# TensorE kept in program order from step 20 on, global softmax moved one and two steps forward

## The chip, the cores and the metric

One core of one Trainium2 chip. The metric is the device time of one execution in microseconds (us), lower is better. The kernel before was measured three times: 1033.65 us median, 1033.2 to 1033.82.

## The reference

Window attention for 8 batches of 8 heads (512 local and 32 global positions, head size 64), then a two-layer FFN (512 to 2048 to 512) with a squared ReLU, in float32:

```python
s_g = scale * np.matmul(q_g, k_all.transpose(0, 1, 3, 2))      # global rows see all 544 keys
out_g = np.matmul(sm(s_g), v_all)
s_ll = np.where(mask, scale * np.matmul(q_l, k_l.transpose(0, 1, 3, 2)), -1e9)   # |i - j| <= 32
a_l = sm(np.concatenate([scale * np.matmul(q_l, k_g.transpose(0, 1, 3, 2)), s_ll], axis=-1))
out_l = np.matmul(a_l, np.concatenate([v_g, v_l], axis=2))
x = np.concatenate([out_g, out_l], axis=2)                     # then to (batch * seq, 512)
h = x @ w_in
r = np.maximum(h, 0.0)
return (s * (r * r) + b) @ w_out
```

## The kernel before, in words

Most operands are split into a high and a low part in the matmul format fp32r, and a product is the sum of three (high by high, high by low, low by high). The work is a software pipeline of 138 steps (the loop at L617). A **head** step `j` (0 to 127) is one head of one half of one batch: 16 steps make a batch, 8 steps make a **tile** of 256 rows of x. An **FFN** step `m = j - 10` takes an eighth of the hidden layer of tile `m // 8`. So step `j` issues, in program order:

- `sp(j+1)`, `ld(j+2)`, `vl(j)`: the splits of K and Q of the next head (L201 to L204, on ScalarE, VectorE and GpSimd) and the loads. K and Q of two heads share one buffer, so in odd steps two copies of K and one or two of Q come together.
- `sc(j)`: four score products into `ps_s` (L383), one for the global queries into `ps_g` (L389), the softmax (L224 on VectorE, L230 on ScalarE, L233 to L240 on VectorE) and the eviction of `ps_g` (L393, L394).
- `early`: in two steps of each batch four transposes of global probabilities into `ps_tg` (L462), evicted by L465 on ScalarE and L466 on VectorE.
- `ffn_in(m)`: 24 products into `ps_h` (L532), then L538, L539, L546, L547 make the hidden values `g` from it.
- `transposes_and_pv(j-1, j-2)`: four transposes into `ps_t` (L324, evicted by L399 and L400) between four products of probabilities and V into `ps_o` (L410, evicted by L421, L422, L424 into the tile `x`).
- `extra`: global softmax (L446 to L451), global V loads (L471) and global products (`g_pv`, ten L484).
- `x_split` (L504, L505) in the last step of a tile, in two halves; the second half of the tile is needed by the seventh and eighth product of `ffn_in` in the next step.
- `ffn_out(m-1)`: 12 products into the two accumulators (L564); after eight of them the tile is copied (L572) and stored.
- `late`: the fifth global transpose of a group (L462 again).

The PSUM tag `t` has one buffer: `ps_t`, `ps_tg` and `ps_xg` take turns in it, and each has to be evicted by ScalarE and VectorE before the next is written. `ps_h` has two buffers; the tags `s`, `g` and `o` have one. The SBUF tag `r` has two, shared by `r`, the stored tiles `o` and the loads `xgr`.

The 17th tile is the global rows. They are written to DRAM by `g_pv` and read back by `xg_split` (L512, two loads of 256 rows, transposed by L515, evicted by L517 and L518), which the program places right behind `ffn_in(127)` and ahead of `ffn_out(126)`.

The loop order is not the engines' order: a scheduler that plays the program on its own cost model orders the instructions of each engine, and moves an instruction forward when its inputs are ready in that model. It is entered by

```python
with _tile.TileContext(nc, schedule_with_timeline_sim=True) as tc:
```

and the steps at which the global softmax of the two groups of four heads is issued, and what follows it, are set by

```python
G_AT = (13, 18)
G_TR = 3
G_LD = (0, 2)
G_PV = (1, 3)
```

so that group `g` of batch `b` has its softmax in step `16*b + G_AT[g]`, its transposes three steps later and its two `g_pv` one and three steps after those.

Of the kernel before, what the change touches and what calls it, by code (L numbers as in the profile page):

```python
# [48 lines left out]
LAG = 10  # L49
# [5 lines left out]
SPOTS = ["xs0", "xs1", "kq", "kq"] * 2 + ["xs1", "kq", "kq"] * 2 + ["xs1", "kq"]  # L55
LOADS_AT = {0: (0, 1), 1: (2, 3), **{j: (j + 2,) for j in range(2, 14)}}
BY_HALVES = 2
NORM_ACT = lambda j: j < 0
X_ACT = lambda j: j >= 8
G_AT = (13, 18)  # L60
G_TR = 3
G_LD = (0, 2)
G_PV = (1, 3)
# [9 lines left out]
def window_attention_then_ffn(ctx: ExitStack, tc: tile.TileContext, qd, qg, kw, vw, vg, qz, qgz, vz, w_in, w_out, sv, bv, out):  # L73
# [63 lines left out]
    def weight_load(k):  # L137
        st = ops.tile([P, 2048], I32, tag=SPOTS[k], name=f"wst{k}", bufs=1 + (SPOTS[k] == "kq"))
        staged[k] = st
        sources = (w_in[k], w_out[k * P:(k + 1) * P, :])  # L140
        for i in range(2):
            queue = nc.scalar if k == 0 else nc.sync
            queue.dma_start(st[:, 1024 * i:1024 * (i + 1)], sources[i])

    def weight_chunk(k):
        st = staged.pop(k)
        n = 2 if k < BY_HALVES else 1
        for i in range(n):
# [66 lines left out]
    def softmax(j, p_s):  # L215
# [19 lines left out]
        for blk in range(2):  # L235
            p = sm[:, cols[blk]]
            if NORM_ACT(j):
                nc.scalar.activation(out=p, in_=p, func=AF.Copy, scale=ss[:, blk:blk + 1])
# [203 lines left out]
    def g_softmax(b, g):  # L442
        v = st_["sg", b, g]
        gm = sb.tile([P, 2], F32, tag="gm", name=f"gm{b}_{g}", bufs=1)
        gm, gs = gm[:, 0:1], gm[:, 1:2]
        nc.vector.reduce_max(out=gm, in_=v, axis=mybir.AxisListType.X)  # L446
        nc.vector.tensor_scalar_mul(gm, gm, -scale)
        nc.scalar.activation(out=v, in_=v, func=AF.Exp, bias=gm, scale=scale, accum_out=gs)
        nc.vector.tensor_scalar_add(gs, gs, 1e-9)
        nc.vector.reciprocal(gs, gs)  # L450
        nc.vector.tensor_scalar_mul(v, v, gs)  # L451
# [132 lines left out]
    NM = NT * 8  # L584
    extra, early, late = defaultdict(list), {}, {}
    for b in range(B):
        for g in range(2):
            s0 = 16 * b + G_AT[g]
            extra[s0].append(lambda b=b, g=g: g_softmax(b, g))
# [23 lines left out]
    piece, last = 0, None  # L613
    qg_load(0)
    ld(0)
    ld(1)
    for j in range(NM + LAG + 2):  # L617
        sp(j + 1)
        ld(j + 2)
        vl(j)  # L620
        for k in LOADS_AT.get(j, ()):
            weight_load(k)
        if j < 16:
            weight_chunk(j)
            piece += 1
        if j < NS:
            b1 = j // 16 + 1
            if j == 14 and NF > 16:
                qg_load32(1)
            elif j % 16 == 14 and b1 < B:  # L630
                qg_load(b1)
            sc(j)
            if j == NF - 1 and NF % 16:
                if NF > 16:
                    qg_load(j // 16)
                qg_split(j // 16)
            if j % 16 == 15 and NF <= j + 1 < NS:
                qg_split(b1)
        if j in early:
            early.pop(j)()  # L640
        m = j - LAG if LAG <= j < NM + LAG else None
        if m is not None:
            ffn_in(m)
            if m == 8 * 15 + 7:
                xg_split(16)
        tr(j - 1)
        transposes_and_pv(j - 1, j - 2)
        vsp(j - 1)
        for fn in extra.pop(j, []):
            fn()  # L650
        pvs(j - 2)
        vl32(j)
        if j in SPLIT_AT:
            x_split(SPLIT_AT[j])
        if last is not None:
            ffn_out(last)
        last = m
        if j in late:
            late.pop(j)()
    assert piece == 16 and not extra  # L660


# [76 lines left out]
```

## Time and profile before

| what | value |
|---|---|
| median of three runs | 1033.65 us |
| time of the profiled execution | 1033.77 us |
| its span in the trace | 1032.0 us |
| TensorE matmul busy | 1009.5 us (98%), 7100 instructions |
| VectorE, ScalarE busy | 801.1 us (78%), 712.3 us (69%) |
| GpSimd busy | 314.7 us (30%) |
| mean granted TensorE clock | 0.993 |

Around the span lie 1.77 us that the trace doesn't show. Matmuls are pipelined: the duration of one is longer than the distance to the next, so distances between starts are the measure of what a product costs.

### The profile page before, as it was taken

How to read it: one execution, taken by the hardware profiler on the slowest of the kernel's cores; microseconds unless marked ns; L12 is line 12 of the kernel's file. 1: busy time of each engine (PE TensorE's matmuls, PEld its weight loads, DVE VectorE, ACT ScalarE, POOL GpSimd, SP SyncE). 2: the span in 40 equal slices, each digit the busy share in tenths (PEclk: the TensorE clock that was granted, in tenths of full speed). 3: DMA queues.
4: the chain of work that ended last, by engine and by line, in shares of the span. 5: the costliest groups of instructions: out<-in, count | busy, mean ns of one | idle time of the engine just before them, and what ended most of it. 6: DMA issues, size and time to landing. Idle time of an engine off the chain costs nothing.

```text
span 1032.0 us, 20335 instructions
## 1 busy us (share of the span) xinstructions
PE 1009.5 (98%) x7100; PEld 915.7 (89%) x7100; DVE 801.1 (78%) x2069; ACT 712.3 (69%) x1775; POOL 314.7 (30%) x365
## 2 busy tenths in 40 slices
PE   9799999999999999999999999999999999999996
PEld 4589999999999899999999999999999989999895
DVE  5899778988799688988799788988799788954321
ACT  7899767867687667867687667868687667844231
POOL 0003233424244234424244234424343234301000
PEclk9899999999999999999999999999999999999999
DMA  8874312312132122312132122312132212201000
GB/s 332 280 260 161 101 51 72 103 48 92 50 109 76 44 73 72 103 48 91 52 107 78 58 64 67 111 40 93 61 98 77 65 57 68 70 1 49 22 21 21
DMA packets 63534, 88.88 MB, mean 86 GB/s; under 512 B 7624, under 2 KB 48584, under 8 KB 63432
## 3 DMA queue, kind: packets, MB, share of 16 engines
q1 hardware_dynamic: 63144, 86.54, 26.3%
q8 instruction: 56, 0.92, 0.4%
q10 hardware_dynamic: 288, 1.05, 0.3%
q14 instruction: 46, 0.38, 0.1%
HBM read 78.12 MB, written 9.44 MB: 85 GB/s over the span
## 4 chain that ended last, share of the span: by engine, by line
PE 87%; ACT 5%; DVE 4%; DMA 2%; issue 1%; SPq 0%; POOL 0%; ACTq 0%; POOLq 0%; DVEq 0%
PE acc L564 36%; PE ps_h L532 33%; PE ps_t L324 5%; PE ps_o L410 4%; PE ps_s L383 4%; PE ps_og L484 2%; ACT sm L230 1%; PE ps_g L389 1%; DMA wst<-in_w_in 1%; DVE sm L240 1%; PE ps_tg L462 1%; PE ps_o L348 1%; ACT wup L158 1%; ACT wst L159 1%; ACT kq L201 0%
## 5 line engine op out<-in xcount | busy, mean ns | idle before, releaser
L532 PE MATMUL ps_h<-xst,w_all 128*128 128x256 f32 x3264 | 437.4, 281 | 4.0 <-ACT xst L504 1.7
L564 PE MATMUL acc<-w_all,g 128*128 128x512 f32 x1632 | 426.9, 397 | 0.0
L532 PEld LDWEIGHTS ps_h<-xst,w_all 128*128 128x128 f32 x3264 | 407.3, 188 | 14.5 <-DVE r L539 2.3
L564 PEld LDWEIGHTS acc<-w_all,g 128*128 128x128 f32 x1632 | 289.7, 188 | 49.1
L212 POOL TENSOR_TENSOR vs<-rv,vs 128x256 fp32r<-128x256 f32 x112 | 85.7, 765 | 274.0 <-ACT vs L211 262.8
L204 POOL TENSOR_TENSOR kq<-rq,kq 128x256 fp32r<-128x256 f32 x112 | 97.7, 872 | 167.2 <-ACT kq L203 159.1
L539 DVE SCALAR_TENSOR_TENSOR r<-ps_h,s_t,r 128x512 f32<-128x512 f32 x136 | 101.2, 744 | 59.7 <-ACT r L538 59.3
L538 ACT ACTIVATE r<-ps_h 128x512 f32<-128x512 f32 x136 | 81.3, 597 | 80.3 <-PE ps_h L532 74.2
L546 ACT ACTIVATE g<-r,b_t 128x512 fp32r<-128x512 f32 x136 | 98.9, 727 | 50.9 <-DVE r L539 49.3
L547 DVE SCALAR_TENSOR_TENSOR g<-r,b_t,g 128x512 fp32r<-128x512 f32 x136 | 106.5, 783 | 33.7 <-ACT g L546 29.9
L230 ACT ACTIVATE sm<-sm,nm 128x224 f32<-128x224 f32 (+1 forms) x256 | 118.6, 467 | 18.8 <-DVE nm L224 17.5
L224 DVE CUSTOM_DVE_ANT_0 sm<-ps_s,mask 128x224 f32<-128x224 f32 (+1 forms) x256 | 85.0, 366 | 19.6 <-PE ps_t L324 10.2
L202 POOL TENSOR_TENSOR kq<-rk,kq 64x416 fp32r<-64x416 f32 x56 | 67.2, 1199 | 106.5 <-DMA wst<-in_w_out 84.6
L324 PE MATMUL ps_t<-ident,sm 128*128 128x128 f32 x512 | 95.4, 279 | 1.7 <-ACT pt L334 1.5
L240 DVE TENSOR_SCALAR sm<-sm,nm 128x224 f32<-128x224 f32 (+1 forms) x256 | 93.4, 405 | 3.7
L410 PE MATMUL ps_o<-pt,vs 128*128 128x256 f32 x448 | 83.3, 280 | 0.0
L476 POOL TENSOR_TENSOR vsg<-rvg,vsg 128x320 fp32r<-128x320 f32 x64 | 57.5, 918 | 75.7 <-ACT vsg L475 75.6
L383 PE MATMUL ps_s<-kq 128*128 128x192 f32 (+1 forms) x448 | 76.4, 276 | 0.6 <-DVE nm L224 0.6
L399 ACT CAST pt<-ps_t 128x416 fp32r<-128x416 f32 x112 | 57.3, 511 | 24.2 <-PE ps_t L324 23.5
L383 PEld LDWEIGHTS ps_s<-kq 128*128 128x128 f32 x448 | 67.4, 190 | 6.2 <-DVE nm L224 0.8
L393 ACT COPY tg<-ps_g 32x256 f32<-32x256 f32 (+1 forms) x112 | 42.2, 377 | 44.1 <-PE ps_g L389 41.8
L394 DVE TENSOR_TENSOR sg<-ps_g,tg 32x256 f32<-32x256 f32 (+1 forms) x112 | 48.1, 429 | 29.7 <-ACT tg L393 23.1
(71 smaller groups left out, 1218.4 us busy)
## 6 DMA issues: line engine op xcount, KB each, us to landing
rq<-in_qd SPq DMA_DIRECT2D x112, 128.0 KB, 2.1
rv<-in_vw SPq DMA_DIRECT2D x112, 128.0 KB, 2.0
rk<-in_kw SPq DMA_DIRECT2D x64, 208.0 KB, 2.5
rvg<-in_vg SPq DMA_DIRECT2D x32, 320.0 KB, 3.0
out<-o SPq DMA_DIRECT2D x34, 256.0 KB, 2.3
wst<-in_w_in SPq DMA_DIRECT2D x15, 512.0 KB, 4.1
wst<-in_w_out SPq DMA_DIRECT2D x15, 512.0 KB, 5.7
rv<-in_vz SPq DMA_DIRECT2D x16, 256.0 KB, 4.6
```

The costliest lines, as they stand in the source:

```text
L204: nc.gpsimd.tensor_sub(out=qs[:, 1, :], in0=rq, in1=f32(qs[:, 0, :]))
L212: nc.gpsimd.tensor_sub(out=vs[:, :, 1, :], in0=rv4, in1=f32(vs[:, :, 0, :]))
L230: nc.scalar.activation(out=p, in_=p, func=AF.Exp, bias=nm[:, blk:blk + 1], scale=-1.0, accum_out=ss[:, blk:blk + 1],)
L240: nc.vector.tensor_scalar(out=p, in0=p, scalar1=ss[:, blk:blk + 1], scalar2=1.0, op0=ALU.mult, op1=ALU.mult,)
L324: nc.tensor.transpose(out=p_t[:, at:at + P], in_=sm[:, c0:c0 + P], identity=ident)
L383: nc.tensor.matmul(p_s[:, cols], lhsT=qs[:, a, blk * P:(blk + 1) * P], rhs=ks[:, cols], start=(a == 0), stop=(a == 1),)
L410: nc.tensor.matmul(p_o[:, blk, :, q0:q0 + n], lhsT=vs[:, 2 * blk + c], rhs=pt[:, :, o], start=(c == 1), stop=(c == 0),)
L532: nc.tensor.matmul(p_h[:, k], lhsT=wi[:, a, f, c], rhs=xs[:, e, c, :], start=(n == 0), stop=(n == 11),)
L539: nc.vector.scalar_tensor_tensor(out=r, in0=p_h, scalar=s_t, in1=r, op0=ALU.mult, op1=ALU.mult)
L546: nc.scalar.activation(out=g[:, 0], in_=r, func=AF.Identity, bias=b_t)
L547: nc.vector.scalar_tensor_tensor(out=g[:, 1], in0=r, scalar=b_t, in1=f32(g[:, 0]), op0=ALU.add, op1=ALU.subtract,)
L564: nc.tensor.matmul(oacc[t][i], lhsT=g[:, a, k, i * P:(i + 1) * P], rhs=wo[:, e, f, :], start=(pr == 0 and n == 0), stop=(pr == 7 and n == 5),)
```

## The change

Two things. First, `G_AT` becomes `(12, 16)`: the softmax of the first group of a batch and all that hangs on it come one step earlier, those of the second group two steps. Second, from step 20 on all that a step puts on TensorE keeps the order in which the program writes it; the other engines' orders are still made by the scheduler. A product no longer passes one that the program wrote ahead of it. No instruction is added or removed. In the changed file the lines behind L57 have numbers higher by one.

```diff
+ORDERED_FROM = 20
-G_AT = (13, 18)
+G_AT = (12, 16)
...
-    for j in range(NM + LAG + 2):
+    def step(j):
+        nonlocal piece, last
         sp(j + 1)
         ld(j + 2)
         vl(j)
...
+
+    for j in range(ORDERED_FROM):
+        step(j)
+    with tc.manual_schedule(engines={mybir.EngineType.PE}):
+        for j in range(ORDERED_FROM, NM + LAG + 2):
+            step(j)
```

The order of TensorE around the four global transposes of a batch's first group, before. The first number in a name is its step: `ps_s49` are the scores of head 49, `ps_h38` the hidden products of FFN step 38 (in step 48), `ps_o46` the products with V of head 46; `ps_tg2_0_0` are the first four transposes of batch 2, group 0, `ps_tg2_0_4` the fifth, and `ps_t46` and `ps_t47` the transposes of heads 46 and 47, which need the same buffer:

```order
L462 MATMUL ps_tg2_0_0_4448<-ident_58,sg32_2796 128x128 x4
L532 MATMUL ps_h38_4455<-xst4_3823,w_all_60 128x256 x8
L410 MATMUL ps_o46_4486<-pt46_4398,vs46_4401 128x256
L410 MATMUL ps_o46_4486<-pt46_4398,vs46_4401 128x2x96
L410 MATMUL ps_o46_4486<-pt46_4398,vs46_4401 128x256
L410 MATMUL ps_o46_4486<-pt46_4398,vs46_4401 128x2x64
L564 MATMUL acc4_0_4020<-w_all_60,g37_4381 128x512 x6
L564 MATMUL acc4_1_4021<-w_all_60,g37_4381 128x512 x6
L383 MATMUL ps_s49_4538<-kq48_4321 128x192 x2
L383 MATMUL ps_s49_4538<-kq48_4321 128x224 x2
L532 MATMUL ps_h39_4558<-xst4_3823,w_all_60 128x256 x4
L324 MATMUL ps_t47_4489<-ident_58,sm47_4337 128x128 x4
```

The same four transposes now:

```order
L390 MATMUL ps_g47_4337<-kq46_4136,qgs2_2703 64x288
L463 MATMUL ps_tg2_0_0_4356<-ident_58,sg32_2817 128x128 x4
L533 MATMUL ps_h37_4363<-xst4_3825,w_all_60 128x256 x24
L411 MATMUL ps_o45_4394<-pt45_4305,vs45_4308 128x256
L411 MATMUL ps_o45_4394<-pt45_4305,vs45_4308 128x2x96
L325 MATMUL ps_t46_4397<-ident_58,sm46_4247 128x128 x2
L411 MATMUL ps_o45_4394<-pt45_4305,vs45_4308 128x256
L411 MATMUL ps_o45_4394<-pt45_4305,vs45_4308 128x2x64
L325 MATMUL ps_t46_4397<-ident_58,sm46_4247 128x128 x2
L565 MATMUL acc4_0_4022<-w_all_60,g36_4288 128x512 x6
L565 MATMUL acc4_1_4023<-w_all_60,g36_4288 128x512 x6
L463 MATMUL ps_tg2_0_4_4433<-ident_58,sg32_2817 128x128
```

They now stand in step 47, ahead of all 24 hidden products; before they stood in step 48, ahead of the last 8 of 24. The next transposes into their buffer are now those of head 46, two products with V behind the run of 24, and the fifth global transpose stands right behind the run of 12. Before, the next ones (head 47) came behind four products with V, a run of 12, four scores and four hidden products.

On ScalarE the eviction of those four transposes (`pg2_0`, from `ps_tg2_0_0`), before:

```order
L546 ACTIVATE g37_4381<-r37_4378,b_t_88 128x512
L393 COPY tg48_4443<-ps_g48_4431 32x256
L230 ACTIVATE sm48_4433,nm48_4434<-sm48_4433,nm48_4434 128x192
L230 ACTIVATE sm48_4433,nm48_4434<-sm48_4433,nm48_4434 128x224
L465 CAST pg2_0_4447<-ps_tg2_0_0_4448 128x16x32
L538 ACTIVATE r38_4480<-ps_h38_4455 128x512
```

and now:

```order
L394 COPY tg47_4349<-ps_g47_4337 32x288
L373 CAST qgs3_4352<-rqg3_4238 128x8x32
L202 CAST kq50_4555<-rk50_4441 64x416
L204 CAST kq50_4555<-rq50_4443 128x256
L202 CAST kq50_4555<-rk50_4441 64x416
L231 ACTIVATE sm47_4339,nm47_4340<-sm47_4339,nm47_4340 128x224
L466 CAST pg2_0_4355<-ps_tg2_0_0_4356 128x16x32
L231 ACTIVATE sm47_4339,nm47_4340<-sm47_4339,nm47_4340 128x192
L449 ACTIVATE sg36_3269,gm2_1_4536<-sg36_3269,gm2_1_4536 128x544
```

Before, it followed both exponentials (L230) of head 48, an even head. Now it follows the first exponential of head 47, an odd one, with the copy of the next batch's global queries (L373 of the changed file) and three copies of K and Q (L202, L204) between it and the eviction of `ps_g47`.

On TensorE at the end of tile 15, where the global rows come back from DRAM (`ps_xg0`, `ps_xg1`), before:

```order
L532 MATMUL ps_h127_13201<-xst15_12784,w_all_60 128x256 x24
L564 MATMUL acc15_0_12912<-w_all_60,g126_13169 128x512 x6
L564 MATMUL acc15_1_12913<-w_all_60,g126_13169 128x512 x6
L515 MATMUL ps_xg0_13235<-ident_58,xgr0_13233 128x128 x4
L564 MATMUL acc15_0_12912<-w_all_60,g127_13229 128x512 x2
L564 MATMUL acc15_1_12913<-w_all_60,g127_13229 128x512 x2
L564 MATMUL acc15_0_12912<-w_all_60,g127_13229 128x512 x4
L564 MATMUL acc15_1_12913<-w_all_60,g127_13229 128x512 x4
L515 MATMUL ps_xg1_13244<-ident_58,xgr1_13242 128x128 x4
L532 MATMUL ps_h128_13263<-xst16_13232,w_all_60 128x256
```

and now:

```order
L533 MATMUL ps_h127_13203<-xst15_12800,w_all_60 128x256 x24
L516 MATMUL ps_xg0_13237<-ident_58,xgr0_13235 128x128 x4
L516 MATMUL ps_xg1_13246<-ident_58,xgr1_13244 128x128 x4
L565 MATMUL acc15_0_12929<-w_all_60,g126_13188 128x512 x6
L565 MATMUL acc15_1_12930<-w_all_60,g126_13188 128x512 x6
L533 MATMUL ps_h128_13265<-xst16_13234,w_all_60 128x256 x24
L565 MATMUL acc15_0_12929<-w_all_60,g127_13231 128x512 x6
```

Both groups of transposes of global rows now stand in a row behind `ps_h127`, ahead of the products of `g126`; before, the products of `g126` and `g127` stood ahead of and between them.

## The prediction

> **What bounds the kernel now.** I read the page first: span, busy times and the chain that ended last.
>
> ```profile
> span 1032.0 us, 20335 instructions
> PE 1009.5 (98%) x7100; PEld 915.7 (89%) x7100; DVE 801.1 (78%) x2069; ACT 712.3 (69%) x1775; POOL 314.7 (30%) x365
> PE 87%; ACT 5%; DVE 4%; DMA 2%; issue 1%; SPq 0%; POOL 0%; ACTq 0%; POOLq 0%; DVEq 0%
> ```
>
> TensorE is busy for 98% of the span and carries 87% of the chain, so what counts is TensorE's own time and the little that it waits. Next come the waits of TensorE and its timeline. Once in 16 steps it stops for a moment at the first products of a tile (us in total, times, longest); two of its rows there, three batches apart, also measure a batch (start, duration, and in brackets the idle time ahead of it):
>
> ```profile
> PE ps_h L532 <- DVE r L539: 1.1, 7, 0.2
> ```
>
> ```profile
> 303.00 2.78 PE L532 MATMUL ps_h<-xst,w_all 128*128 128x256 f32 x22 [0.17 <-DVE r L539]
> ```
>
> ```profile
> 650.45 1.80 PE L532 MATMUL ps_h<-xst,w_all 128*128 128x256 f32 x13 [0.16 <-DVE r L539]
> ```
>
> Three batches take 650.45 - 303.00 = 347.45, or 115.8 us each, and of such waits there are seven in the whole trace, 1.1 us together: before, TensorE almost never waits in the middle. Now the steps that already stand in program order, 46 and 47 (scores, hidden products, products with V, run of 12, next scores):
>
> ```profile
> 319.42 0.58 PE L383 MATMUL ps_s<-kq 128*128 128x224 f32 x4
> ...
> 326.34 0.58 PE L383 MATMUL ps_s<-kq 128*128 128x224 f32 x4
> 326.76 0.30 PE L389 MATMUL ps_g<-kq,qgs 128*64 128x288 f32 x1
> 326.90 2.91 PE L532 MATMUL ps_h<-xst,w_all 128*128 128x256 f32 x24
> 329.64 0.38 PE L410 MATMUL ps_o<-pt,vs 128*128 128x256 f32 x2
> 329.86 0.38 PE L324 MATMUL ps_t<-ident,sm 128*128 128x128 f32 x2
> ...
> 330.41 3.00 PE L564 MATMUL acc<-w_all,g 128*128 128x512 f32 x12
> 333.24 0.60 PE L383 MATMUL ps_s<-kq 128*128 128x192 f32 x4
> ```
>
> They take 6.92 and 6.90 us from scores to scores.
>
> **The change, part by part.** *Runs in place of mixtures.* From step 20 on every head step looks like these two. The rest of a batch is four groups of ten global products and ten global transposes:
>
> ```profile
> 354.35 0.76 PE L484 MATMUL ps_og<-vsg,pg 128*64 128x128 f32 x10
> 354.95 0.45 PE L532 MATMUL ps_h<-xst,w_all 128*128 128x256 f32 x2
> ```
>
> ```profile
> 335.64 0.60 PE L462 MATMUL ps_tg<-ident,sg 128*128 128x128 f32 x4
> 335.99 1.19 PE L532 MATMUL ps_h<-xst,w_all 128*128 128x256 f32 x8
> ```
>
> Ten products take 0.60, four transposes 0.35 (0.09 each). A batch in order is 16 x 6.91 + 4 x 0.60 + 10 x 0.09 = 113.9. The first product behind such a group comes late by nothing to 0.11 (no row shows all cases), for six groups nothing to 0.7; I take 0.3: 114.2. That is 1.6 less than 115.8. Steps 20 to 127 are 6.75 batches: **-10.9 us** (-8.2 to -12.8), the small waits of before being in it. It holds while TensorE finds its inputs ready, and in program order it has nothing else to do when one is late. So I looked for buffers that the order asks for early.
>
> *One buffer for three kinds of transposes.* In step 16b+15 four global transposes go ahead of the 24 hidden products, and the four of a head follow two products with V later, in the same buffer. From the start of the scores TensorE is there after 0.42 (326.76) + 0.14 (326.90) + 0.35 for the global transposes + 0.11 + 2.74 (329.64 less 326.90) + 0.22 (329.86) = 3.98. By then ScalarE (L465) and VectorE (L466) must have evicted them. ScalarE's queue in step 47 of before is that of the changed kernel but for the eviction itself, which now stands behind the first exponential; its timeline:
>
> ```profile
> 327.10 0.39 ACT L393 COPY tg<-ps_g 32x288 f32<-32x288 f32 x1 [1.60 <-PE ps_g L389]
> ...
> 329.14 0.48 ACT L230 ACTIVATE sm<-sm,nm 128x224 f32<-128x224 f32 x1
> 329.44 1.31 POOL L202 TENSOR_TENSOR kq<-rk,kq 64x416 fp32r<-64x416 f32 x1
> ...
> 329.62 0.44 ACT L230 ACTIVATE sm<-sm,nm 128x192 f32<-128x192 f32 x1
> ...
> 330.18 0.60 DVE L233 TENSOR_SCALAR nm<-nm 128x2 f32<-128x2 f32 x1 [0.19 <-ACT sm L230]
> ...
> 332.41 0.83 DVE L451 TENSOR_SCALAR sg<-sg,gm 128x544 f32<-128x544 f32 x1
> ...
> 333.50 0.57 DVE L400 TENSOR_TENSOR pt<-ps_t,pt 128x416 fp32r<-128x416 f32 x1
> ...
> 334.10 0.42 DVE L424 TENSOR_TENSOR x<-u 64x256 f32<-64x256 f32 x1
> ...
> 336.73 0.59 ACT L465 CAST pg<-ps_tg 128x512 fp32r<-128x512 f32 x1
> ...
> 337.62 0.68 DVE L466 TENSOR_TENSOR pg<-ps_tg,pg 128x512 fp32r<-128x512 f32 x1
> ```
>
> The second exponential begins at 329.62, 3.28 after the scores; the eviction now has that place: 3.28 + 0.59 + 0.68 + about 0.1 between engines = 4.65. TensorE stands for 0.7. Behind the run of 12 it wants the buffer again, for the fifth global transpose, at 4.65 + 0.55 + 2.83 = 8.0. L400 ended at 334.07 there, 7.73 after the scores; with the eviction ahead of it (0.45 on ScalarE) 8.2: a wait of 0.2 (0 to 0.6). In step 16b+19, the second group, the copy of the global queries (0.3) is not there but two stores of the tile end in ScalarE's queue just ahead: about 0.2 earlier, a wait of 0.5. Both kinds of step have their crowd (K and Q copies of coming heads) in batches 1 to 6 only. 6 x (0.7 + 0.2 + 0.5) = **+8.4 us** (0, if ScalarE gets there 0.7 sooner, to 16).
>
> *The end of a tile.* Fourteen tiles (2 to 15) begin in the ordered part. The second half of `x_split` hangs on L424 of the last head and is needed by product 8 of the next `ffn_in`, at 6.91 + 0.56 + 7 x 0.114 (2.74 / 24) = 8.27. In step 47 L424 ended at 334.52, 8.18 after the scores, behind a global softmax that these steps don't have (L451 with its neighbours, about 1.0): 7.2. Then the split itself:
>
> ```profile
> L505 DVE TENSOR_TENSOR xst<-x,xst 128x512 fp32r<-128x512 f32 x32 | 22.1, 691 | 5.1 <-ACT xst L504 5.1
> L504 ACT CAST xst<-x 128x512 fp32r<-128x512 f32 x32 | 19.7, 617 | 10.5 <-DVE x L424 10.1
> ```
>
> 7.2 + 0.62 + 0.69 + 0.05 = 8.5 to 8.6: late by about 0.25 (0 to 0.7), 14 times: **+3.5 us** (0 to 9.8). Part of what makes it late is VectorE beside GpSimd: the one small L233 of 330.18 took 0.60 while L202 ran on GpSimd (its group's mean is 226 ns). [...]
>
> *The global rows at the end.* The chain as it ran before (the load L512 is issued by SP):
>
> ```profile
> 966.29 0.75 DVE L547 SCALAR_TENSOR_TENSOR g<-r,b_t,g 128x512 fp32r<-128x512 f32 x1 [0.16 <-ACT g L546]
> 967.07 6.71 SPq L512 DMA_DIRECT2D xgr<-xg_d  x2
> 970.09 2.88 PE L564 MATMUL acc<-w_all,g 128*128 128x512 f32 x12
> 972.82 0.60 PE L515 MATMUL ps_xg<-ident,xgr 128*128 128x128 f32 x4
> ...
> 977.46 0.50 PE L532 MATMUL ps_h<-xst,w_all 128*128 128x256 f32 x2 [0.67 <-ACT xst L517]
> 978.18 7.54 PE L532 MATMUL ps_h<-xst,w_all 128*128 128x256 f32 x64 [0.22 <-DVE xst L518]
> ```
>
> ```profile
> DMA to landing us min/median/max: 2.6/2.6/2.7
> ```
>
> Both loads use one buffer: the second is issued (973.4, the end of the merged row) when the first has been transposed, and lands 2.6 later, at 976.0, under a run of 12. Now nothing of TensorE stands between the two groups of transposes. The first load is released by L547 (966.29 + 0.75 = 967.04), which was 3.05 ahead of the end of the hidden products (970.09) and is 2.45 ahead now, since the ten global products (0.60) no longer stand in that step; so it lands 0.2 to 0.4 late. Then come 0.44 of transposes, about 0.25 until they are done and 2.65 for the second load: TensorE idles about 0.4 + 2.9 = 3.3, where before it idled 0.67 + 0.22 = 0.9: **+2.4 us**. What else hung on the loads (the evictions L517, L518) is hidden by the products of step 126, 2.8 long. Such a stop has a second price, the granted clock:
>
> ```profile
> 27.00:30.50 3.50, 1.77 (x9) 1.24 (x8) 3.48 (x9) 3.12 (x10) 0.00 (x0) 1.00 0.88 279
> 30.50:34.00 3.50, 1.88 (x9) 1.24 (x8) 3.37 (x9) 3.50 (x7) 0.00 (x0) 0.54 1.00 383
> 34.00:37.40 3.40, 3.40 (x15) 3.07 (x13) 2.39 (x9) 3.40 (x8) 0.00 (x0) 0.50 0.38 133
> ```
>
> In these windows (first number: length; second: TensorE busy; the clock is the third from the end) TensorE was idle for 1.73 of 3.5 us, and the clock fell to half for the next 6.8. A stop of 2.9 can do the same; half the clock for 3.4 to 6.8 us costs 1.7 to 3.4, and nothing if it doesn't come. I take **+1.7 us** (0 to 3.4). [...] The rows above show that 1.73 of idleness sufficed, so the measurement decides.
>
> *The global softmax one and two steps sooner* adds no instruction. What moves with it are 32 loads on SP's queue, 64 copies with as many subtractions on GpSimd (30% busy) and 32 small stores; their queues have room, and they keep three steps, 20 us, from softmax to transposes. I cost it at nothing; if a load came late, a group of products would wait for up to its landing, about 3 us, in place of passing it. It is in the upper end.
>
> **The sum**, against the profiled execution (1033.77; the median of the three runs is 1033.65, the same within 0.12): 1033.77 - 10.9 + 8.4 + 3.5 + 2.4 + 1.7 = **1038.9 us**. What a measurement here can tell from no change is 0.2%, 2.07 us.
>
> **The rivals.**
>
> *The evictions come in time.* If ScalarE reaches the eviction 0.7 sooner and the splits are ready, what is left is 1033.77 - 10.9 + 2.4 + 1.7 = 1027.0. For it: the two waits are 0.5 to 0.7 beside chains of 4.6, and the tile's 0.25 is within what a row scatters. Against: ScalarE worked without a gap from 327.10 to 329.62. It decides at the point where all repeated waits together fall below 4.7 us. Chance 0.27.
>
> *Half of them.* Repeated waits of 4.7 to 8.8 us, mainly the first groups' 0.7: 1031.7 to 1035.8, about 1033.7, no change. Chance 0.16, with the case that the order is kept and nothing else moves (the order of TensorE's instructions shows runs of 24 and 12 from step 20 on, so that the change does not do what it says is out but for a part of it).
>
> *ScalarE and VectorE become the bound.* In the steps with a softmax of a global group, their work plus evictions outlasts the step and TensorE waits for L400, L539 and L224 as well; twice the 8.4 and twice the 3.5: 1050.8. For it: L400 ended 7.73 after the scores in step 47, beyond the step's 6.90. Against: the next steps have 0.5 to 1 us of room each. Chance 0.08.
>
> **How the numbers follow.** The forecast, repeated waits of 8.8 to 18 us, has 0.49; then 0.27, 0.16 and 0.08. Faster is the first rival, 0.27; same the second, 0.16; slower forecast and third, 0.57. The range leaves out the lowest part of the first rival (1025.3 with no slow clock) and the highest of the third: 1027 to 1048. It is no narrower since the repeated waits, each worked out to some 0.4, come 32 times.
>
> **What would show it.** Right: TensorE waits at L324 (0.4 to 0.7 in steps 16b+15 and 16b+19, released by VectorE's L466), at product 7 or 8 of a tile's first hidden products, and once about 3 us at L515 with a half clock behind it; a batch of 114 plus its waits, near 116. Wrong: no idle rows at L324 and a batch of 114.2, then it is the first rival; new waits at L383, L389 or L564, then the third; a batch without waits that is still 115.8, then the gain of runs was mine alone.

## The result, and the profile after

The changed kernel takes 1044.31 us (median of four runs, 1043.72 to 1046.94), the kernel before 1033.74 on the same chip: a ratio of 1.0101 with a 95% interval of 1.0089 to 1.0114. By the ratio it is 10.4 us slower, where 5.1 were forecast. The profiled execution took 1046.94, 2.6 above its own median; its first L565 comes at 69.63 where the profile of before has L564 at 67.50, though both run the same 300 products up to there. So 2.1 us of the difference between the two profiled executions lie ahead of anything that the change touches.

The page of the kernel after, its span, its busy times and its chain:

```profile
span 1045.1 us, 20292 instructions
PE 1012.5 (97%) x7100; PEld 918.4 (88%) x7100; DVE 779.8 (75%) x2069; ACT 715.8 (68%) x1775; POOL 327.9 (31%) x365
PE 89%; ACT 5%; DVE 3%; DMA 2%; issue 0%; POOL 0%; SPq 0%; DVEq 0%; ACTq 0%; POOLq 0%
```

TensorE is busy for 3.0 us more than before, and its span is 13.1 longer: in the rest it stands. What it waited for from 190 us on (us in total, times, longest):

```profile
PE ps_t L325 <- DVE pg L467: 6.3, 12, 0.6
PE ps_xg L516 <- DVE xst L519: 2.9, 1, 2.9
PE ps_h L533 <- DVE xst L506: 0.3, 1, 0.3
PE ps_xg L516 <- DMA xgr<-xg_d: 0.2, 1, 0.2
```

The first line is the wait that the prediction put at steps 16b+15 and 16b+19. It comes twelve times, twice in each of six batches. The third line stands for a wait that shows more in the distances between products than here. A batch, from the first L564 (L565) of one FFN step to that of the sixteenth behind it, in the windows of the two kernels (each begins and ends 0.2 us ahead of that product; length, then TensorE, its weight loads, VectorE, ScalarE and GpSimd, the clock third from the end):

```profile
537.58:653.04 115.46, 115.30 (x837) 106.67 (x836) 97.01 (x259) 84.13 (x223) 43.68 (x50) 1.00 0.25 75
```

```profile
540.78:657.22 116.44, 115.41 (x836) 106.58 (x835) 93.45 (x259) 84.71 (x222) 45.35 (x50) 1.00 0.25 74
```

The prediction had 114.2 and its waits, near 116. Over the five batches from FFN step 32 to 112 the mean is 115.78 before (one of the five took 116.72) and 116.48 after.

Step 16b+15, the one whose sum the prediction worked out (all lines behind L57 are higher by one now, so that the prediction's L324, L465 and L466 are L325, L466 and L467):

```profile
331.61 0.58 PE L384 MATMUL ps_s<-kq 128*128 128x224 f32 x4
...
332.17 0.60 PE L463 MATMUL ps_tg<-ident,sg 128*128 128x128 f32 x4
...
334.40 0.48 ACT L231 ACTIVATE sm<-sm,nm 128x224 f32<-128x224 f32 x1
...
335.00 0.59 ACT L466 CAST pg<-ps_tg 128x512 fp32r<-128x512 f32 x1
...
335.43 0.37 PE L411 MATMUL ps_o<-pt,vs 128*128 128x256 f32 x2
...
335.62 0.69 DVE L467 TENSOR_TENSOR pg<-ps_tg,pg 128x512 fp32r<-128x512 f32 x1 [0.36 <-ACT pg L466]
...
336.36 0.33 PE L325 MATMUL ps_t<-ident,sm 128*128 128x128 f32 x1 [0.56 <-DVE pg L467]
```

The eviction begins behind the first exponential, 3.39 after the scores (forecast 3.28), and TensorE goes on 4.75 after them (forecast 4.65). TensorE would have been there 4.03 after them (forecast 3.98). By the distances of the products the wait is 0.72 in step 16b+15 and 0.62 to 0.72 in 16b+19. The start of a tile (VectorE's half of the split, and TensorE's weight loads that wait for it):

```profile
180.87 0.68 DVE L506 TENSOR_TENSOR xst<-x,xst 128x512 fp32r<-128x512 f32 x1
...
181.61 0.99 PEld L533 LDWEIGHTS ps_h<-xst,w_all 128*128 128x128 f32 x8 [0.20 <-DVE xst L506]
```

The product there comes 0.17 late, and the next one 0.11 more: 0.28. It is 0.24 to 0.28 at twelve tiles, 0.54 at one and nothing at the last, tile 15: 3.8 together (forecast 0.25 at fourteen, 3.5). And the end:

```profile
976.40 3.71 SPq L513 DMA_DIRECT2D xgr<-xg_d  x2
...
979.09 0.66 PE L516 MATMUL ps_xg<-ident,xgr 128*128 128x128 f32 x4 [0.19 <-DMA xgr<-xg_d]
979.62 0.75 DVE L540 SCALAR_TENSOR_TENSOR r<-ps_h,s_t,r 128x512 f32<-128x512 f32 x1 [3.25 <-ACT r L539]
980.41 0.72 ACT L547 ACTIVATE g<-r,b_t 128x512 fp32r<-128x512 f32 x1 [0.82 <-DVE r L540]
981.04 0.57 ACT L518 CAST xst<-ps_xg 128x512 fp32r<-128x512 f32 x1
981.16 0.75 DVE L548 SCALAR_TENSOR_TENSOR g<-r,b_t,g 128x512 fp32r<-128x512 f32 x1 [0.79 <-ACT g L547]
981.83 0.68 DVE L519 TENSOR_TENSOR xst<-ps_xg,xst 128x512 fp32r<-128x512 f32 x1
982.61 1.08 PE L516 MATMUL ps_xg<-ident,xgr 128*128 128x128 f32 x4 [2.86 <-DVE xst L519]
983.34 5.39 PE L565 MATMUL acc<-w_all,g 128*128 128x512 f32 x12
```

The stop is as long as forecast (2.9 and 0.2), but two things end it within a tenth of a microsecond: the second load, issued at 979.8 and 2.6 to 2.7 under way, and the eviction L519, which ended at 982.51. The run of 12 behind it took 5.39, where the prediction's rows have 2.88 and 3.00: half the clock.

### The profile page after: what moved, and what is told of

It is laid out like the page before. It is cut to its first block, busy times and chain, and to the rows that moved or that the text cites. A ratio compares the mean times of both kernels' runs of the same rounds, so it can differ in the third digit from the quotient of the medians.

```text
span 1045.1 us, 20292 instructions
## 1 busy us (share of the span) xinstructions
PE 1012.5 (97%) x7100; PEld 918.4 (88%) x7100; DVE 779.8 (75%) x2069; ACT 715.8 (68%) x1775; POOL 327.9 (31%) x365
## 4 chain that ended last, share of the span: by engine, by line
PE 89%; ACT 5%; DVE 3%; DMA 2%; issue 0%; POOL 0%; SPq 0%; DVEq 0%; ACTq 0%; POOLq 0%
PE acc L565 36%; PE ps_h L533 34%; PE ps_t L325 6%; PE ps_s L384 4%; PE ps_o L411 4%; PE ps_og L485 2%; PE ps_g L390 1%; DMA wst<-in_w_in 1%; PE ps_o L349 1%; DVE pg L467 1%; ACT sm L231 1%; ACT pg L466 1%; ACT kq L202 1%; ACT wup L159 1%; ACT wst L160 1%; PE ps_tg L463 1%
## 5 line engine op out<-in xcount | busy, mean ns | idle before, releaser
L565 PE MATMUL acc<-w_all,g 128*128 128x512 f32 x1632 | 413.8, 400 | 0.0
L533 PE MATMUL ps_h<-xst,w_all 128*128 128x256 f32 x3264 | 409.3, 280 | 2.2 <-ACT xst L505 1.9
L533 PEld LDWEIGHTS ps_h<-xst,w_all 128*128 128x128 f32 x3264 | 392.8, 189 | 7.5 <-DVE xst L506 2.8
L565 PEld LDWEIGHTS acc<-w_all,g 128*128 128x128 f32 x1632 | 297.5, 189 | 56.6 <-DVE g L548 0.3
L548 DVE SCALAR_TENSOR_TENSOR g<-r,b_t,g 128x512 fp32r<-128x512 f32 x136 | 104.4, 768 | 21.8 <-ACT g L547 12.9
L547 ACT ACTIVATE g<-r,b_t 128x512 fp32r<-128x512 f32 x136 | 99.4, 731 | 17.5 <-DVE r L540 15.2
L325 PE MATMUL ps_t<-ident,sm 128*128 128x128 f32 x512 | 99.2, 281 | 10.7 <-DVE pg L467 7.9
L477 POOL TENSOR_TENSOR vsg<-rvg,vsg 128x320 fp32r<-128x320 f32 x64 | 77.2, 1225 | 48.2 <-ACT vsg L476 48.1
L203 POOL TENSOR_TENSOR kq<-rk,kq 64x416 fp32r<-64x416 f32 x56 | 62.9, 1123 | 91.9 <-DMA wst<-in_w_out 87.0
L234 DVE TENSOR_SCALAR nm<-nm 128x2 f32<-128x2 f32 x128 | 41.0, 320 | 63.6 <-ACT sm L231 63.6
L241 DVE TENSOR_SCALAR sm<-sm,nm 128x224 f32<-128x224 f32 (+1 forms) x256 | 72.8, 327 | 4.0
L325 PEld LDWEIGHTS ps_t<-ident,sm 128*128 128x128 f32 x512 | 55.3, 142 | 15.2 <-DVE pg L467 8.2
L401 DVE TENSOR_TENSOR pt<-ps_t,pt 128x416 fp32r<-128x416 f32 x112 | 65.5, 585 | 3.0 <-ACT pt L400 1.7
```

What stands on the lines that cost most here:

```text
L325: nc.tensor.transpose(out=p_t[:, at:at + P], in_=sm[:, c0:c0 + P], identity=ident)
L533: nc.tensor.matmul(p_h[:, k], lhsT=wi[:, a, f, c], rhs=xs[:, e, c, :], start=(n == 0), stop=(n == 11),)
L547: nc.scalar.activation(out=g[:, 0], in_=r, func=AF.Identity, bias=b_t)
L548: nc.vector.scalar_tensor_tensor(out=g[:, 1], in0=r, scalar=b_t, in1=f32(g[:, 0]), op0=ALU.add, op1=ALU.subtract,)
L565: nc.tensor.matmul(oacc[t][i], lhsT=g[:, a, k, i * P:(i + 1) * P], rhs=wo[:, e, f, :], start=(pr == 0 and n == 0), stop=(pr == 7 and n == 5),)
```

## The experiments

Ratios to the kernel before, each measured beside it (its median moved from 1033.7 to 1035.1 between the chips and hours, so what is compared below is ratios, at 10.34 us for each 0.01):

| kernel | median, us | ratio, 95% interval |
|---|---|---|
| changed kernel | 1044.31 | 1.0101, 1.0089 to 1.0114 |
| softmax sooner only | 1040.32 | 1.0059, 1.0047 to 1.0072 |
| globals ahead of the scores | 1054.63 | 1.0195, 1.0181 to 1.0209 |
| end apart | 1039.62 | 1.0050, 1.0036 to 1.0064 |
| stop filled | 1043.75 | 1.0091, 1.0077 to 1.0104 |
| loads apart | 1042.51 | 1.0070, 1.0057 to 1.0083 |
| tile start | 1041.87 | 1.0066, 1.0052 to 1.0080 |
| globals in `h` from batch 1 | 1036.54 | 1.0023, 1.0011 to 1.0034 |
| order from step 18 | 1044.51 | 1.0093, 1.0078 to 1.0108 |
| all repairs, in order | 1027.09 | 0.9919, 0.9906 to 0.9932 |
| the same, softmax in 11 and 15 | 1039.09 | 1.0045, 1.0032 to 1.0057 |
| all repairs, mixed order | 1026.64 | 0.9922, 0.9910 to 0.9934 |
| all repairs, order from 18 | 1027.21 | 0.9925, 0.9913 to 0.9937 |
| before, with buffers | 1028.85 | 0.9936, 0.9924 to 0.9949 |
| before, with tile start | 1037.33 | 1.0020, 1.0011 to 1.0029 |
| before, with end apart | 1033.65 | 0.9985, 0.9976 to 0.9994 |
| before, with buffers and shift | 1031.61 | 0.9965, 0.9951 to 0.9979 |

**The two parts of the change.** First the shift alone:

```diff
-    for j in range(ORDERED_FROM):
-        step(j)
-    with tc.manual_schedule(engines={mybir.EngineType.PE}):
-        for j in range(ORDERED_FROM, NM + LAG + 2):
-            step(j)
+    for j in range(NM + LAG + 2):
+        step(j)
```

> The softmax of the global rows one and two steps sooner, and nothing in program order: TensorE's whole program is mixed as before. My theory: the shift alone costs nothing and the loss lies in the order; the median is that of the kernel before, 1033.7, within 2 us, and a batch of 16 steps takes 115.4 us as before. Rival 1: the shift is the loss (it puts the softmax and the global transposes into steps where ScalarE and VectorE have more to do); then 1039 to 1044 and a batch of 116.4. Rival 2: the shift is a gain of its own that the order eats up; then below 1031.5.

Measured: 6.1 us slower than before, so rival 1 holds in its number, and the prediction's "I cost it at nothing" falls for the mixed order. TensorE's waits from 190 us on, and a batch:

```profile
PE ps_h L533 <- DVE xst L506: 5.0, 6, 0.9
PE ps_h L533 <- ACT xst L505: 1.1, 3, 0.4
```

```profile
537.47:653.77 116.30, 115.43 (x836) 106.71 (x835) 99.78 (x259) 84.73 (x223) 42.89 (x50) 1.00 0.26 74
```

Once in each of six batches TensorE stops for 0.9 to 1.1 us (by the distances of the products) at the start of the odd tile: in the scheduler's new mixture the split of x comes too late there. The other half, the order with the former steps, has no run. By the program it would stand still: the global rows of step 16b+20 (L395) go into the buffer that the transposes of step 16b+21 still have to read, the scores of step 16b+21 stand ahead of these transposes and need the `ps_g` that L395 has to free, and in program order the transposes can't pass them. If that is so, the shift is also what the order needs.

**The shared buffer.** The global transposes one place further up, at the end of the step before:

```diff
-            early[s0 + G_TR] = lambda b=b, g=g: g_transposes(b, g, 0, 4)
+            late[s0 + G_TR - 1] = lambda b=b, g=g: g_transposes(b, g, 0, 4)
```

> The changed kernel, with the four global transposes at the end of the step before, ahead of the scores in place of behind them, so that ScalarE and VectorE meet their eviction before the softmax of the head. My theory: the waits of TensorE at the head's transposes (0.72 and 0.64 us, twelve of them, 8.2 us) are the late eviction of the one shared buffer, and they go: 1036.1, a batch of 115.1 in place of 116.44. Rival: ScalarE and VectorE are simply behind in these steps, and the wait moves to the next thing that TensorE wants of them (the scores, the global transposes themselves or the products with V): above 1041, a batch above 116.

```profile
PE ps_tg L463 <- DVE pt L401: 4.1, 6, 0.7
...
PE ps_h L533 <- DVE xst L506: 1.0, 2, 0.5
```

```profile
552.41:668.12 115.71, 115.03 (x836) 106.18 (x835) 94.16 (x259) 85.05 (x222) 45.37 (x50) 1.00 0.25 74
```

The median says nothing here: from FFN step 0 to 16 this kernel takes 14.2 us more than the changed one, since the scheduler made another mixture of the first 20 steps, with stops of 5.7 and 2.2 us and half the clock for 13.7. In the ordered part both waits at L325 are gone, and one of them has come back a step earlier, at L463, for the eviction of the head's own transposes: 0.68, six times. A batch gained 0.73 of the 1.34 expected. Moving work within one buffer moved half of the wait. The next kernel leaves the order of TensorE as it is, word for word, and changes the buffer:

```diff
-            p_t = ps.tile([P, 4, P], F32, tag="t", name=f"ps_tg{b}_{g}_{c0}")
+            p_t = ps.tile([P, 4, P], F32, tag="h" if b else "t", name=f"ps_tg{b}_{g}_{c0}", bufs=2 if b else 1)
```

> The changed kernel, with the global transposes of batches 1 to 7 in the pair of PSUM buffers of the hidden products in place of the one that the head's transposes use; order and operations of TensorE are the same. My theory: the twelve waits of 0.72 and 0.64 us are that one buffer and nothing else: 8.2 us less, 1036.1, a batch of 115.1 in place of 116.44. Rival: ScalarE and VectorE are behind in these steps whatever the buffer (as the version with the global transposes ahead of the scores showed for one of the two groups, where 0.68 of wait stayed six times), and TensorE waits for the next thing they deliver: a batch of 115.7 or more, 1040 or more.

```profile
PE ps_xg L516 <- DVE xst L519: 2.9, 1, 2.9
PE ps_h L533 <- DVE xst L506: 0.4, 1, 0.4
```

```profile
650.26:765.31 115.05, 115.04 (x836) 106.57 (x835) 93.44 (x259) 84.46 (x222) 45.41 (x50) 1.00 0.25 75
```

0.0078 below the changed kernel, 8.1 us (expected 8.2), and no wait at L325 from 190 us on. The batch shown is one of five that take 114.98 to 115.68, 115.2 on the mean. The twelve waits are the one buffer, not a backlog of ScalarE and VectorE.

**The tile start.**

```diff
+            if pr == 0 and k == 0 and t >= 2:
+                order = sorted(order, key=lambda x: x[0] >= 2 and x[2])
```

> The changed kernel, with the products of a tile's first 12 (from the third tile on) in another order: those that read the second half of the low part of x last, so that VectorE's half of the split is needed three products (0.34 us) later. My theory: what is lost at the start of each tile (0.17 of wait and 0.11 behind it, by the distances of the products; 14 tiles) is the lateness of that one subtraction: 14 x 0.28 = 3.9 less, 1040.4. Rival: the split is late as a whole or the 0.11 is the price of any change of operand; then a part stays, 1042 to 1043.5.

Measured 3.6 us less by the ratios (expected 3.9); no wait for L506 is left from 190 us on, and batches take 115.85 to 116.2 but for one of 116.74, in which a wait at L463 is new. The theory holds.

**The end.** Loads (tag `rv`) and PSUM (tags `t` and `s`) apart:

```diff
-            xr = sb.tile([P, DM], F32, tag="r", name=f"xgr{i}", bufs=2)
+            xr = sb.tile([P, DM], F32, tag="rv", name=f"xgr{i}")
-            p_t = ps.tile([P, 4, P], F32, tag="t", name=f"ps_xg{i}")
+            p_t = ps.tile([P, 4, P], F32, tag="ts"[i], name=f"ps_xg{i}")
```

> The changed kernel, with the two loads of the global rows at the end in two buffers of their own and their transposes in two PSUM buffers that are free by then. My theory: the stop of 2.9 us at 979.8 goes and with it the half clock of 6.8 us behind it, that cost 3.2 by the distances of the products: 1044.3 - 2.9 - 3.2 = 1038.2. Rival 1: the half clock has another cause and stays: 1041.4. Rival 2: the stop has a third cause (the hidden products of step 126 or the evictions) and stays in part: 1042 or more.

Measured 5.3 us less (expected 6.1). In the profile the stop and the half clock are gone, and FFN steps 120 to 128 take 46.72 in place of 52.98 (48.24 before). Only the first of the two edits:

> The changed kernel, with the two loads of the global rows at the end in two buffers of their own, their transposes still in one PSUM buffer. The prediction's reason for the stop of 2.9 us was the second load, which waits for the first transposes and takes 2.65. By it, the stop shrinks to the eviction of the first transposes alone, worked out there to be hidden: 1044.3 - 2.9 = 1041.4, and 1040 or less with the slow clock gone too. Rival, from the trace of the changed kernel: ScalarE and VectorE had the hidden products' own four operations (L539, L540, L547, L548) ahead of the eviction (L518, L519), which ended at 982.51, 0.1 us behind the landing of the load; the buffer in PSUM is then as late as the load, and the time is that of the changed kernel, 1043.7 to 1044.5, with the stop still 2.7 or more.

```profile
PE ps_xg L516 <- DVE xst L519: 1.7, 1, 1.7
```

Measured 3.2 us less, so the rival is out, and the prediction's reason is a part of it: the stop shrank from 2.9 to 1.7 and no further. But the run changed two things: with the load early, the scheduler also put the eviction (L518, L519) ahead of L547 and L548. What is left is the eviction alone; how much of the 1.2 was the load and how much the new place of the eviction isn't shown, since in the changed kernel both ended the stop together. The clock stayed full at the end (1.00 from 975.80 to 986.10). Last the stop kept as it is, and filled with 25 products that nobody reads:

```diff
+            if i == 0:
+                p_w = ps.tile([P, 512], F32, tag="s", name="fill")
+                for _ in range(25):
+                    nc.tensor.matmul(p_w[:, 0:224], lhsT=masks[False][:, 0:P], rhs=masks[False], start=True, stop=True)
```

> The changed kernel, with 25 products of 128x224 in bf16, whose result nobody reads, on TensorE between the two groups of transposes at the end: about 2.5 us of work inside the stop of 2.9, so that the stop lasts as long as before but TensorE isn't idle in it. My theory: the idleness is what halves the clock, so that the clock stays full and the time falls by the 3.2 us that the slow products cost: 1041.1. Rival: the clock falls to half for another reason (the end of the dense part, ScalarE's or VectorE's share) and the time stays 1044.3 or rises by what the filling is late.

```profile
979.72 2.56 PE L520 MATMUL fill<-mask 128*128 128x224 bf16 x25
982.77 0.66 PE L516 MATMUL ps_xg<-ident,xgr 128*128 128x128 f32 x4 [0.49 <-DVE xst L523]
```

(L523 is L519 in this file.) In this profile the clock stays full at the end (1.00 from 974.31 to 984.54), and FFN steps 124 to 128 take 26.55 in place of 29.35. So idleness it is. But the ratios differ by 1.0 us only, not by 3.2. Half clock isn't bound to this stop: in this trace it came at 139.8, for 3.4 us, behind the stop of the next paragraph, and FFN steps 0 to 16 took 123.6 in place of the changed kernel's 121.7; the same shows with the loads apart and with the tile start. And the price of one stop isn't the same in each run: those of the changed kernel had a mean granted clock of 0.989 (the profiled one), 0.991, 0.992 and 0.992, and between the first and the last lie, by an estimate, 2 x 0.003 x 1044 = 6 us at half clock.

**The seam.** The changed kernel also stopped for 1.6 us at 138.7, where the mixed and the ordered part meet: the scheduler had put the fifth global transpose of step 19 just ahead of the head's transposes of step 20.

```diff
-ORDERED_FROM = 20
+ORDERED_FROM = 18
```

> The changed kernel, in program order from the 18th step on in place of the 20th. My theory: the stop of 1.6 to 1.8 us at 138.7 comes from the seam: the scheduler pulls the fifth global transpose of step 19 up to just ahead of the head's transposes of step 20, where its eviction is not done. With the seam ahead of step 19 the stop goes: 1044.3 - 1.8 = 1042.5. Rival: two more steps in order are two more steps of the first tiles in which TensorE waits for weights or inputs in place of passing them; the stop moves and the time is 1044 or more.

The stop went and the time did not (0.8 less, within the intervals): FFN steps 4 to 8 take 1.7 us more in its place. The rival holds.

**All together.** The end apart, the tile start, and the buffers, now for the second group of batch 0 too (`"h" if b or g else "t"`):

> The changed kernel with all repairs together: the global transposes (but for the first group's of batch 0) in the buffers of the hidden products, the products of a tile's first 12 in the later order, loads and transposes of the last rows apart. My theory: the losses are separate and add up: 1044.3 - 7.8 (buffers) - 2.4 (tile start) - 4.7 (end) - 1.6 (the stop at the seam, whose transposes now have a buffer of their own) = 1027.8, a batch of 114.5, which is 0.9 to 1.2 under the mixed order's 115.4 to 115.8. Rival: the losses stand in for one another (with one wait gone the next thing is late): 1031 or more, a batch of 115 or more.

```profile
647.84:762.31 114.47, 114.47 (x836) 106.33 (x835) 93.47 (x259) 84.48 (x222) 45.50 (x50) 1.00 0.26 75
```

0.0081 faster than the kernel before, 0.0182 or 18.8 us faster than the changed one: the losses add up (expected 16.5). Then the same with the softmax in steps 11 and 15 (`G_AT = (11, 15)`):

> The kernel with all repairs, and the global softmax in steps 11 and 15 of a batch in place of 12 and 16. My theory: in program order, with buffers to spare, it doesn't matter in which step the global rows are worked on: the time of the kernel with all repairs within 1 us. Rival: the place matters by itself, as it did by 6 us in the mixed order: 3 us or more above it.

By the median the rival, 12 us slower. But from FFN step 0 to 16 it takes 130.1 us against 120.3, all in the mixed part: one stop of 4.5 us at 120 and half the clock for 10.2 behind it. From FFN step 16 to the end it takes 829.7 against 828.0. So in the ordered part of these two traces the place costs 1.7 us, more than the theory allowed and less than the rival. The order from step 18 on:

> The kernel with all repairs, in program order from step 18 on in place of 20. My theory: with the seam's stop gone already, two more steps in order change nothing that can be told: within 1 us of it. Rival: the seam costs by itself wherever a mixed program meets an ordered one, and steps 18 and 19 in order gain (or lose) 1.5 us or more.

No difference, as expected. And the control, the kernel before with the same three repairs, its own steps and its mixed order:

> The kernel before with the same three repairs, in its mixed order and with its own steps for the global softmax (13 and 18). My theory: the repairs mend what the order brings about, and the order itself is worth 0.9 to 1.2 us a batch, so that the mixed order gains by them only the 0.9 us that it waits at the end: 1033 to 1034.5, 5 us or more above the ordered kernel with all repairs. Rival: the repairs are the gain and the order is worth nothing: 1027 to 1029.5.

```profile
647.10:761.85 114.75, 114.75 (x836) 106.35 (x835) 97.26 (x258) 84.47 (x222) 43.72 (x49) 1.00 0.26 75
```

My theory is out: the mixed order is as fast as the ordered one (0.9922 and 0.9919, each to 0.0013). All its batches take 114.75. In order an undisturbed batch takes 114.47, but from FFN step 16 on three of six take longer, up to 115.44, and the five from step 32 to 112 take 114.72 on the mean. So 0.0 to 0.3 us a batch of order is left, and in the whole kernel nothing that can be told. Which repair did that for the mixed order was then tried one by one, the buffers first:

> The kernel before, mixed order and its own steps, with one of the three repairs alone: the global transposes (but for the first group's of batch 0) in the buffers of the hidden products. My theory: it is this one buffer that made the mixed order dear, since the scheduler has to break runs of products to place three kinds of transposes in it; with two buffers more the order has 160 changes from line to line in a batch in place of 179 and a batch takes 114.8 in place of 115.4 to 115.8: 5 to 7 us less than the kernel before. Rival: the gain of the three repairs in the mixed order came from the tile start or the end, and this alone gives under 2 us.

```profile
645.97:760.63 114.66, 114.66 (x836) 106.27 (x835) 97.66 (x258) 84.42 (x223) 42.88 (x49) 1.00 0.25 75
```

6.6 us faster than the kernel before, as the theory had it, and a batch takes 114.81 on the mean of the five in place of 115.78. The luck of one mixture is no likely rival: the three mixed kernels with these buffers (this one, that with all repairs, and the last one below) take 114.8 to 114.9, the four without them (before, the shift, the tile start, the end apart) 115.7 to 116.7.

The reason within the theory, broken runs, fits less well. Counted in the traces from FFN step 48 to 112, TensorE changes from one line's products to another's 179 times a batch in the kernel before, 161 times here, 160 with all repairs, and 136 times in order. The last 24 changes fewer brought 0.0 to 0.3 us, so 18 fewer don't explain 0.97. TensorE's waits in the same five batches of before are

```profile
PE ps_h L532 <- DVE r L539: 0.8, 5, 0.2
PE ps_s L383 <- DVE nm L224: 0.6, 1, 0.6
PE ps_tg L462 <- DVE pt L400: 0.3, 1, 0.3
```

and here there are none. By the distances of the products they cost more than these rows say: the stop at L532 once in a batch, which the prediction read as 0.16, takes 0.33 and 0.11 more at the next product, and all of them together 3.85 us, or 0.77 a batch. So about 0.7 of the 0.97 are short stops that the mixture with the buffers doesn't have, and the rest may be the fewer changes. Only the waits at L462 are for the shared buffer itself; why the others go with it isn't shown.

The other two:

> The kernel before with another of the three repairs alone: the products of a tile's first 12 in the later order. My theory: TensorE passes the split there already (waits of 1.1 us in the whole trace), so it gains nothing to 1 us. Rival: the late split is what forces the scheduler to mix, and a batch falls to 114.8, 5 us or more less in all.

> The kernel before with the third repair alone: loads and transposes of the last global rows apart. My theory: the idle time there was 0.9 us, and that is the gain, 0 to 1.5 us, with batches as before. Rival: the gain of the repairs in the mixed order sits here, 3 us or more.

The tile start alone gains nothing (2.1 us slower, with another mixture), the end alone 1.6 us, a little more than expected. So the buffers carry it. With the shift on top of it:

> The mixed order with the global softmax one and two steps sooner and the global transposes in the buffers of the hidden products. It tells what the 6 us of the shift alone hung on. My theory: on the one buffer, for which three kinds of transposes crowd when the softmax comes sooner; with the buffers free, the shift costs nothing: the time of the mixed order with these buffers alone, within 1.5 us. Rival: it hangs on the steps themselves (the split of x in step 17 of a batch meets the softmax of step 16 and the loads of step 17), and 4 us or more stay above it.

3.0 us above the mixed order with buffers, between the two expectations: of the 6.1 that the shift cost by itself, about half hung on the buffer, and a batch takes 114.9 instead of 114.8 on the mean. The rest (a stop of 1.1 us at 928 among it) stays open.

## Why the prediction was right in sign and wrong in size

The terms against what the runs showed, in us; the sum is made for the profiled execution, in which the stretch from the first product of L564 to the start of TensorE's last grew from 954.5 to 966.1, by 11.5:

| term | forecast | shown |
|---|---|---|
| runs in place of mixtures | -10.9 | -8.8 = 6.75 x (114.47 - 115.78) |
| the buffer `t`, steps 16b+15 and 16b+19 | +8.4 | +8.1 (buffer alone) |
| end of a tile | +3.5 | +3.6 (order of the products alone) |
| the last rows, stop | +2.4 | +2.1 = 2.86 + 0.19 - 0.9 |
| half the clock behind it | +1.7 | +3.2 in this run, less in the others |
| the seam at step 20 | not seen | +1.6 |
| shift of the softmax | 0 | not separable in order; +6.1 by itself |

The right-hand sum is 9.8 of 11.5; 1.7 stays without a cause. An estimate of where it lies, from the time of each stretch beyond what its products take at their usual distances (226 ns for one of L565, 113 for one of L533, which by themselves last 400 and 280 on the mean, and so on): about 1.0 in the mixed steps ahead of the seam, and about as much in FFN steps 16 to 112, which lost 4.9 where the terms give 3.9.

*Runs in place of mixtures* is the step that failed, in size and in what it took for the cause; with it failed what the sum left out, the seam (1.6), and what it put at half its later size, the clock. In size: "that is 1.6 less than 115.8" was 1.31 for an undisturbed batch in order (and 1.06 on the mean of the kernel with all repairs). Ten global products cost 0.68 and not 0.60; the first product behind a group comes 0.06 late, as priced. In cause: the prediction charged the whole difference to the mixing of products. The mixed order with the buffer free takes 114.81 over the same five batches. So 0.97 of the 1.31 go with one shared buffer, and 0.1 to 0.3 are that of the mixing. The sentence "before, TensorE almost never waits in the middle" was read from the waits' rows; by the distances its stops cost 0.77 a batch. And the prediction used the buffer as a term of the ordered program only, though the mixed program paid for it as well.

*The buffer* was right in place and releaser. That its size came out, 8.1 for 8.4, is in part luck: the second group's 0.5 was 0.62 to 0.72, and the wait of 0.2 at the fifth global transpose did not come, for no row of the trace behind step 20 has it, so two errors cancel. Doing the same work earlier (globals ahead of the scores) brought half of the loss back at L463, which the third rival's argument, L400 late in a crowded step, had seen; the rival itself, twice the waits and new ones at L383 or L564, is not there.

*The tile* was right. *The last rows* were right in length, and half wrong in reason: the second load was taken for what ends the stop and the evictions for hidden, but load and eviction ended it together, and with the load out of the way a stop of 1.7 for the eviction is left. *The clock* came, for 6.8 us in the profiled run, twice the value taken and within its bounds; in four of five profiles with the stop of 2.9 us the clock fell.

*The shift* at nothing was wrong for the mixed program, and what it does in the ordered one is known only as far as 11 and 15 against 12 and 16 show. *The seam* was missed because the sum began at step 20 and the first twenty steps were taken as unchanged. They aren't: an edit elsewhere can make the scheduler mix them anew, and in two of these kernels that cost 10 and 14 us.

## What to carry to other kernels

Ask of a buffer that several kinds of work share what it costs in the order that exists, not only in the order proposed: a scheduler's mixture pays for it too, here in short stops at other places, which the rows of waits show at less than half of their cost, so that distances between products have to be read. One kind of work moved to other buffers was worth more here (6.6 us) than the whole order. An engine held to program order needs each of its buffers free when the program says so (here TensorE stood for 0.62 to 0.72 us at L325, twelve times), and moving a piece of work within the same buffer moves the wait (here to L463, 0.68, six times). Compare an ordered program with the mixed one under the same repairs before the order gets the credit.

## What the runs showed of the hardware

In each trace the changes of the granted clock lie whole multiples of 3.41 us apart: in the changed kernel they come at 32.78, 39.61, 60.09, 63.50, 981.68 and 988.51, whose first and fifth lie 278 windows of 3.413 us apart. So the same stop of 2.9 us cost by how it fell into these windows. In the changed kernel and in that with the globals in `h` (length, TensorE busy, clock third from the end):

```profile
978.27:981.68 3.41, 1.28 (x10) 0.84 (x8) 1.26 (x2) 1.79 (x3) 0.00 (x0) 1.00 0.29 77
981.68:985.09 3.41, 2.48 (x8) 2.22 (x9) 1.53 (x3) 0.59 (x1) 0.00 (x0) 0.50 0.05 19
985.09:988.51 3.42, 3.42 (x9) 2.65 (x9) 0.00 (x0) 0.00 (x0) 0.00 (x0) 0.50 0.02 5
988.51:991.92 3.41, 3.41 (x28) 3.26 (x28) 0.00 (x0) 0.32 (x1) 0.00 (x0) 1.00 0.00 0
```

```profile
969.46:972.88 3.42, 0.52 (x5) 0.31 (x4) 2.10 (x3) 1.39 (x3) 0.00 (x0) 1.00 0.31 77
972.88:976.29 3.41, 3.41 (x11) 2.81 (x10) 0.69 (x1) 0.58 (x1) 0.00 (x0) 0.50 0.02 5
976.29:979.70 3.41, 3.41 (x26) 3.13 (x25) 0.00 (x0) 0.00 (x0) 0.00 (x0) 1.00 0.00 0
```

Where the stop falls into one window, the next is slow and the one behind it full (3.4 us at half clock); where it runs into the slow window and leaves it 2.48 us of work, the one behind that is slow as well, and it is 6.8. With the order from step 18 on the stop fell across two windows, and the clock stayed:

```profile
976.39:979.81 3.42, 1.92 (x15) 1.48 (x14) 0.75 (x1) 1.24 (x3) 0.00 (x0) 1.00 0.18 66
979.81:983.22 3.41, 1.72 (x10) 1.53 (x11) 1.78 (x3) 1.14 (x3) 0.00 (x0) 1.00 0.23 77
```

About half a window of idleness decided. Over all eighteen traces, a window at full clock with at most 1.69 us of TensorE's work was always followed by half the clock, one with 1.77 or more never, and between them (1.70 to 1.76) four were and four were not. The way back asked for more: behind a slow window with up to 2.93 us of work the clock stayed at half, behind one with 3.0 or more it was full, and of two with 2.95 and 2.96 one was.

VectorE became faster in the changed kernel with the same instructions, 779.8 us busy in place of 801.1. One of them, before and after:

```profile
L202 DVE TENSOR_TENSOR kq<-rk,kq 64x416 fp32r<-64x416 f32 x56 | 49.6, 886 | 2.1
```

```profile
L203 DVE TENSOR_TENSOR kq<-rk,kq 64x416 fp32r<-64x416 f32 x56 | 36.0, 643 | 2.1
```

Its mean is 886 ns in the one order and 643 in the other. What decided was whether a GpSimd subtraction was already under way when it began. Where none was (21 of 56 before, 47 of 56 after), it took 584 to 587 ns, though in each of these 68 cases one began beside it within 0.35 us (in one of them 1 ns ahead). Where one was (35 and 9), it took 826 to 1457 ns, and in each of the 44 it ended 443 to 451 ns behind the end of GpSimd's. So in these two traces the one that began first ended first (but for that 1 ns), and the order of the instructions decided which that was. The prediction's small L233 fits: it ended 0.03 us behind the GpSimd instruction beside it.
